# Two blocks through the first product together, with their hidden tiles kept in DRAM

## The chip, the cores and the metric

The kernel runs on one core of a Trainium2 chip. The metric is device time in microseconds (us) of one execution. The engines are named as in the profile: PE (matmuls; PEld is its weight loads), DVE (vector), ACT (scalar), POOL (GpSimd) and SP, whose queue issues nearly all DMAs.

## The reference

Linear attention, a norm over each head, and two feed-forward layers, all in float32 at the end; inputs come as 64-bit floats in DRAM.

```python
kv  = einsum('bhsd,bhse->bhde', k, v)            # 8 batches, 8 heads, 576 rows, 64 columns
out = einsum('bhsd,bhde->bhse', q, kv)
out = out / sqrt(mean(out * out, -1) + 1e-6) * g_norm
x   = out.transpose(0, 2, 1, 3).reshape(4608, 512)
h   = maximum(maximum(x @ w1, x @ w2), x @ w3)   # 512 x 768 each
x1  = h @ w_out                                  # 768 x 512
g   = s * maximum(x1 @ w_in, 0) ** 2 + b         # 512 x 2048
y   = g @ w2_out                                 # 2048 x 512
```

## The kernel before

The 4608 rows are cut into nine blocks of 512 columns (x is kept transposed): block j below 8 holds the first 512 rows of batch j, and block 8 collects the last 64 rows of all eight batches (`o_rem`). The first layer, called first and second product here, is done block by block; the second layer (lines 505 to 851) works on pairs of blocks afterwards with seven products in place of eight, and is not touched.

Every product of two float32 numbers is done as three matmuls of halves: `split` (line 91) writes a rounded high part (ACT, line 92) and the rest (line 93, on DVE or POOL), and `mm3` (line 95) issues the three matmuls (lines 96, 97, 98).

**The first product** of a block has G1 = 18 groups g: output tile m = g // 3 of h and weight matrix g % 3. `g1_part(j, g, kks)` (line 358) runs 4 x 3 = 12 matmuls of 512 columns into one of four PSUM banks of the pool `psg`; `g1_out` (line 365) copies the first of three groups to `h` (ACT) and takes the maximum with the other two (DVE, line 372); `h_split` (line 374) splits h into one of six buffers `HS` (on DVE for block 0 and for the last m, on POOL otherwise). **The second product** (`g2_mm`, line 378) has 4 groups n of 6 x 3 = 18 matmuls, in the same four banks; `g2_out` (line 385) copies them out (ACT) through the two buffers named "st" and stores them to DRAM (`x1d`).

**Weights.** The 18 tiles of w1, w2, w3 and the six of w_out are unpacked from 64-bit floats by integer and float operations: `conv_load` (line 145, DMA of 512 KB by SP), `conv_unpack` (lines 161 to 166: three operations on DVE, three on ACT), `conv_sum` (line 171, POOL), `conv_split` (lines 92 and 93, ACT and DVE). Three sets of buffers (`stages`, line 191) take turns; two of them lie in the slots that the tiles of w_out will fill later (raw tile `raw_o`). The 32 tiles of the second layer's weights pass through one stage and are stored to DRAM (`wd`, lines 496 to 501).

**Attention** of batch bb: `load_kv`, `load_rem`, `load_q`, `kv_mm` (line 243), `kv_diag`, then for each of four pairs of heads p: `q_turn` (transpose on DVE, line 278), `q_split`, `o_mm` (lines 291 to 300), `o_out` (ACT), `plan_norm` (rounding on DVE, line 318; its rest on POOL, line 319; two matmuls, lines 328 and 329; three ACT operations; three on DVE, lines 342 to 344), and `x_split` (line 348) into the block's tiles xh and xl. Batch 0 does o and the norm in full float32 without splits.

**Order.** Each step is put into `plan` with `at(pos, ...)` (line 65); `run` sorts by position and issues in that order. One unit of `pos`, called a slot here, is the time of one group of 12 matmuls; `us(t)` turns planned microseconds into slots (1 / 2.6 slot each, with t = 28 at slot 0). From slot 20 on the order on PE and SP is the planned one; below 20 only SP's, and the other engines' orders, PE's included, come from the framework's scheduling of the program. A block takes SL = 22 slots. In slots 0 to 22 block 0 runs its 18 groups, then its second product, and so on with block j from slot 22 j; batch j + 1's attention is planned beside block j. Weight tiles are planned from us(3) on, 2.6 to 3.5 planned us apart, and those of w_out 5 apart; k and v of batches 1, 2 and 3 are planned at us(19), us(34) and us(49), so ahead of slot 10.

Of the kernel before, what the change touches and what calls it, by code (L numbers as in the profile page):

```python
# [9 lines left out]
F32 = mybir.dt.float32  # L10
F32R = mybir.dt.float32r
# [9 lines left out]
P = 128  # L21
N = 512
# [7 lines left out]
def attention_max_ffn_relu2_ffn(ctx: ExitStack, tc, q, k, v, g_norm, w1, w2, w3, wo, wi, w2o, s, b, out):  # L30
# [34 lines left out]
    def at(pos, fn, *args):  # L65
        plan.append((pos, len(plan), fn, args))
# [279 lines left out]
    xs = {}  # L346

    def x_split(j, p, eng):
        if p == 0:
            xs[j] = (base.tile([P, KD, N], F32R, tag="xh", name=f"xh_{j}"),  # L350
                     base.tile([P, KD, N], F32R, tag="xl", name=f"xl_{j}"))
        split(xs[j][0][:, p], xs[j][1][:, p], st["o", j, p], eng)

# [1 line left out]

    def g1_part(j, g, kks):
        if kks[0] == 0:
            st["g1", g] = psg.tile([P, N], F32, tag="g", name=f"g1_{j}_{g}")  # L360
        xh, xl = xs[j]
        for kk in kks:
            mm3(st["g1", g], wt["w", g], slice(kk * P, (kk + 1) * P), xh[:, kk], xl[:, kk], kk == 0, kk == KD - 1)

    def g1_out(j, g):
        m, i = divmod(g, 3)
        ps = st.pop(("g1", g))
        if i == 0:
            st["h", m] = ttile(f"h_{j}_{m}")
            act(out=st["h", m], in_=ps, func=AF.Copy)  # L370
        else:
            nc.vector.tensor_tensor(out=st["h", m], in0=ps, in1=st["h", m], op=ALU.max)  # L372
# [48 lines left out]
    for p in range(NP):  # L421
# [16 lines left out]
    stages_o = [stages[0], stage(HS[M1 - 1], HS[M1 - 2], "st")]  # L438
    pos = us(3)
    for n in range(G1 + M1):  # L440
        step = 2.6 if n < 3 else 3.5 if n < 6 else 2.6 if n < 22 else 5
        plan_conv(n, pos, US)
        pos += step * US

    for j in range(NB):
        t = SL * j
        if j + 1 < B:
            bb = j + 1
            xpb = 3 if j else 2
            if bb < 4:  # L450
                kt = us(4 + 15 * bb)
                plan_kv(bb, lambda p: kt + (2 * p - 3.9) * US, lambda p: kt + 2 * p * US)
            else:
                plan_kv(bb, lambda p: t - 4 + p - 1.9, lambda p: t - 4 + p + 0.5)
            at(max(t - 10, us(20)), load_q, bb, 0, NP)
            at(t + 0.2, kv_diag, bb)
            for p in range(NP):
                a = t + 3 * p
                at(a + 0.4, q_turn, bb, p)
                if bb:  # L460
                    at(a + 1.3, q_split, bb, p)
# [3 lines left out]
                at(t + G1 + 0.2 + 0.5 * p, x_split, bb, p, nc.gpsimd if p < xpb else nc.vector)  # L465
            at(t + 13.3, o_rems, bb)
        elif j + 1 == B:
            for p in range(NP):
                a = t + 3 * p

                def sq(p=p):
                    st["o", B, p] = o_rem[:, p, :]
                    o_sq(B, p, o_rem[:, p, :])

                at(a + 0.4, sq)
                plan_norm(B, p, a + 0.5, 0.9)
                at(t + G1 + 0.2 + 0.5 * p, x_split, B, p, nc.gpsimd if p < 3 else nc.vector)
        for g in range(G1):
            if j or g >= 4:
                at(t + g, g1_part, j, g, range(KD))  # L480
            at(t + max(g, j == 0 and 3 or 0) + 1.01, g1_out, j, g)
            if g % 3 == 2:
                at(t + max(g, j == 0 and 3 or 0) + 1.25, h_split, j, g // 3)
        for n in range(KD):
            if j:
                if n < 2:
                    at(t + G1 + max(n, 0.3), g2_mm, j, n, range(M1 - 1))
                    at(t + G1 + 1.8 + 0.01 * n, g2_mm, j, n, [M1 - 1])
                else:
                    at(t + G1 + n, g2_mm, j, n, range(M1))  # L490
            at(t + G1 + max(n + 1.01, 2.01 + 0.1 * n) if j else t + G1 + 3 + 0.3 * n, g2_out, j, n)
        if not j:
            for m in range(M1):
                for n in range(KD):
                    at(t + G1 + 0.3 + m * 0.5 + 0.01 * n, g2_mm, j, n, [m])
# [383 lines left out]
```

## Time and profile before

| | |
|---|---|
| median of 3 runs | 1455.7 us (1454.43 to 1456.37) |
| profiled execution, first to last instruction (span) | 1453.9 us |
| around the span, if the profiled execution took the median's time | 1.8 us |
| PE busy (matmuls) | 1396.9 us, 96% |
| DVE busy | 951.2 us, 65% |
| ACT busy | 813.8 us, 56% |
| POOL busy | 332.7 us, 23% |
| moved by DMA | 202.63 MB, 139 GB/s in the mean |

The profiled execution's time is known by its span alone. Shares are means over the whole program; the page's second part cuts the span into 40 slices of 36 us and gives each engine's busy share in tenths (9 is 90% or more). The other views used are the stretches (busy time of each engine between two times, the granted clock of PE as a share of full speed, and the mean share of time that the DMA engines are busy, which can come out a little above 1), the timelines of single engines, and groups of instructions by line and tile. In a row of a group "x12 | 11.2, 933" means twelve instructions, 11.2 us together, 933 ns each, and behind the second bar the idle time ahead of them and what ended it.

### The profile page before, as it was taken

How to read it: one execution, taken by the hardware profiler on the slowest of the kernel's cores; microseconds unless marked ns; L12 is line 12 of the kernel's file. 1: busy time of each engine (PE TensorE's matmuls, PEld its weight loads, DVE VectorE, ACT ScalarE, POOL GpSimd, SP SyncE). 2: the span in 40 equal slices, each digit the busy share in tenths (PEclk: the TensorE clock that was granted, in tenths of full speed). 3: DMA queues.
4: the chain of work that ended last, by engine and by line, in shares of the span. 5: the costliest groups of instructions: out<-in, count | busy, mean ns of one | idle time of the engine just before them, and what ended most of it. 6: DMA issues, size and time to landing. Idle time of an engine off the chain costs nothing. (4 is left out here: it accounts for less than half of the span.)

```text
span 1453.9 us, 19580 instructions
## 1 busy us (share of the span) xinstructions
PE 1396.9 (96%) x6860; PEld 1145.0 (79%) x6860; DVE 951.2 (65%) x1439; ACT 813.8 (56%) x1454; POOL 332.7 (23%) x238
## 2 busy tenths in 40 slices
PE   4689999999999999999999999999999999999997
PEld 2467888888878788888878778988788888888887
DVE  4899473646364636446466765756877888888785
ACT  5776454445353545443365646647676666656565
POOL 1334242324232324331100000000002414141412
PEclk9789999999999999999999999999999999999999
DMA  9986244435364742213135464453676444454541
GB/s 195 198 207 106 76 65 111 111 117 102 127 91 124 113 123 58 80 29 116 65 124 202 162 230 178 142 203 127 217 265 231 132 146 174 152 175 148 176 135 40
DMA packets 229459, 202.63 MB, mean 139 GB/s; under 512 B 126320, under 2 KB 179568, under 8 KB 227184
## 3 DMA queue, kind: packets, MB, share of 16 engines
q1 hardware_dynamic: 229200, 201.11, 48.9%
q8 instruction: 54, 0.88, 0.3%
q14 instruction: 45, 0.37, 0.1%
q10 hardware_dynamic: 160, 0.26, 0.0%
HBM read 126.88 MB, written 74.45 MB: 138 GB/s over the span
## 5 line engine op out<-in xcount | busy, mean ns | idle before, releaser
L97 PE MATMUL g<-xl,w_w 128*128 128x512 f32 x648 | 255.9, 395 | 3.8 <-POOL xl L93 3.8
L96 PE MATMUL g<-xh,w_w 128*128 128x512 f32 x648 | 257.4, 400 | 0.2 <-ACT xh L92 0.2
L98 PE MATMUL g<-xh,w_w 128*128 128x512 f32 x648 | 255.6, 395 | 0.0
L92 ACT ACTIVATE zx<-z 128x512 fp32r<-128x512 f32 (+1 forms) x280 | 161.2, 586 | 123.5 <-PE zs_a L707 35.7
L629 PE MATMUL ps_a<-x_q,w_q 128*128 128x512 f32 (+1 forms) x960 | 211.1, 371 | 2.8 <-DVE cs L537 1.7
L707 PE MATMUL zs_a<-zx,w_q 128*128 128x512 f32 (+1 forms) x960 | 203.7, 369 | 0.6 <-POOL zx L93 0.3
L93 POOL TENSOR_TENSOR zx<-z,zx 128x512 fp32r<-128x512 f32 (+1 forms) x46 | 63.3, 1376 | 593.8 <-DMA gd<-cs 381.4
L629 PEld LDWEIGHTS ps_a<-x_q,w_q 128*128 128x128 f32 x960 | 167.2, 188 | 38.0 <-DVE cs L537 3.4
L93 DVE TENSOR_TENSOR zx<-z,zx 128x512 fp32r<-128x512 f32 (+1 forms) x234 | 170.6, 746 | 34.8 <-ACT zx L92 34.3
L707 PEld LDWEIGHTS zs_a<-zx,w_q 128*128 128x128 f32 x960 | 167.8, 188 | 31.9 <-POOL zx L93 0.7
L97 PEld LDWEIGHTS g<-xl,w_w 128*128 128x128 f32 x648 | 123.3, 190 | 29.7 <-POOL xl L93 4.2
L96 PEld LDWEIGHTS g<-xh,w_w 128*128 128x128 f32 x648 | 123.2, 191 | 26.8 <-issue 1.0
L98 PEld LDWEIGHTS g<-xh,w_w 128*128 128x128 f32 x648 | 123.2, 190 | 26.3
L171 POOL TENSOR_TENSOR tr_ctr<-tr_ctr,gc_cgc 128x512 int32<-128x512 int32 x42 | 56.0, 1333 | 232.4 <-DVE gc_cgc L166 169.8
L629 PE MATMUL ps_b<-x_q,w_q 128*128 128x512 f32 (+1 forms) x480 | 107.6, 372 | 1.1 <-ACT cs L640 1.0
L707 PE MATMUL zs_b<-zx,w_q 128*128 128x512 f32 (+1 forms) x480 | 103.8, 371 | 2.2 <-DVE zx L93 2.2
L372 DVE TENSOR_TENSOR h<-g,h 128x512 f32<-128x512 f32 x108 | 73.9, 684 | 42.9 <-PE g L98 42.4
L707 PEld LDWEIGHTS zs_b<-zx,w_q 128*128 128x128 f32 x480 | 83.9, 188 | 19.1 <-DVE zx L93 3.4
L629 PEld LDWEIGHTS ps_b<-x_q,w_q 128*128 128x128 f32 x480 | 83.8, 188 | 18.9 <-ACT cs L640 1.8
L96 PE MATMUL g<-h,w_o 128*128 128x512 f32 x216 | 85.7, 397 | 0.0
L162 ACT ACTIVATE tr_ctr<-raw_craw 128x512 int32<-128x512 uint32 x42 | 28.1, 669 | 102.1 <-DMA wd<-tr_ctr 86.1
L97 PE MATMUL g<-h,w_o 128*128 128x512 f32 x216 | 84.6, 392 | 0.0
(160 smaller groups left out, 2268.3 us busy)
## 6 DMA issues: line engine op xcount, KB each, us to landing
z<-gd SPq DMA_DIRECT2D x64, 512.0 KB
gd<-cs SPq DMA_DIRECT2D x96, 256.0 KB
z<-gd SPq DMA_DIRECT2D x48, 256.0 KB
x1d<-x SPq DMA_DIRECT2D x36, 256.0 KB
k<-in_k_dram SPq DMA_DIRECT2D x32, 256.0 KB
v<-in_v_dram SPq DMA_DIRECT2D x32, 256.0 KB
raw_craw<-in_moe_w_in_dram SPq DMA_DIRECT2D x16, 512.0 KB
wd<-tr_ctr SPq DMA_DIRECT2D x32, 256.0 KB
```

Of the source, the lines that this page charges most:

```text
L92: act(out=hi, in_=src, func=AF.Copy)
L93: eng.tensor_tensor(out=lo, in0=src, in1=hi.bitcast(F32), op=ALU.subtract)
L96: nc.tensor.matmul(ps, lhsT=w[:, 0, sl], rhs=xh, start=first, stop=False)
L97: nc.tensor.matmul(ps, lhsT=w[:, 0, sl], rhs=xl, start=False, stop=False)
L98: nc.tensor.matmul(ps, lhsT=w[:, 1, sl], rhs=xh, start=False, stop=last)
L162: act(out=r, in_=w32[:, :, 0], func=AF.Copy, scale=2.0 ** -29)
L171: nc.gpsimd.tensor_tensor(out=t, in0=t, in1=g.bitcast(I32), op=ALU.add)
L372: nc.vector.tensor_tensor(out=st["h", m], in0=ps, in1=st["h", m], op=ALU.max)
L629: nc.tensor.matmul(ps, lhsT=w[:, a, c], rhs=x[:, b_], start=new and k == 0 and e == 0, stop=k == HK - 1 and e == 2, skip_group_check=True)
L707: nc.tensor.matmul(ps, lhsT=w[:, a, c], rhs=x[:, b_, :n], start=new and k_ == 0 and e == 0, stop=k_ == 3 and e == 2, skip_group_check=True)
```

## The change

Blocks 0 and 1 go through the first product together. Block 0 runs groups 0 to 6 alone (`LEAD = 7`), then the groups of block 1 and of block 0 take turns (block 1's g at slot 7 + 2 g, block 0's g at 2 g - 6), until block 0 is through at slot 29; block 1's last seven groups follow to slot 36. Each finished h tile of both blocks is stored to DRAM (`h_store`, into `hd`). From slot 36 the second products of block 0 and of block 1 follow, four slots each, with m in the outer loop: their h tiles are loaded back about three slots ahead (`h_load`) and split on DVE. Block 2 begins at slot 44 as before.

With it go: block 0's x lies in four of the six `HS` buffers (block 1's in xh and xl as before), and block 1's h in the other two; the attention of batch 1 is planned at us(28) to us(46), ahead of slot 10, with its x splits on DVE, and that of batch 2 at slots 14 to 36; k and v of batches 2 and 3 are loaded beside blocks 1 and 2 in place of the head. Of the weight tiles only 0 to 3 are planned at the old pace, 4 and 5 at us(22) and us(26), tile n from 6 on four slots ahead of block 0's group n, and w_out's every two slots from slot 27. The second layer's unpacking starts at slot 44 - 2.5 in place of 28 - 2.5, spaced 4.05 in place of 4.5 slots.

```diff
+    hd = [dram.tile([P, M1, N], F32, name=f"hd{j}") for j in range(2)]
...
     def x_split(j, p, eng):
+        if not j:
+            x = pair(HS[p], f"x_{p}")
+            xs[j, p] = (x[:, 0], x[:, 1])
...
     def g1_out(j, g):
...
         if i == 0:
-            st["h", m] = ttile(f"h_{j}_{m}")
+            st["h", j, m] = ttile(f"h_{j}_{m}") if j != 1 else base.tile([P, 2, N], F32, tag=HS[M1 - 2 + m % 2],
+                                                                         name=f"h_{j}_{m}")[:, 0]
...
+    def h_store(j, m):
+        nc.sync.dma_start(out=hd[j][:, m], in_=st["h", j, m])
+
+    def h_load(j, m):
+        st["h", j, m] = (ttile if m % 2 else stile)(f"hl_{j}_{m}")
+        nc.sync.dma_start(out=st["h", j, m], in_=hd[j][:, m])
...
-        split(h[:, 0], h[:, 1], st["h", m], nc.vector if m == M1 - 1 or j == 0 else nc.gpsimd)
+        split(h[:, 0], h[:, 1], st["h", j, m], nc.vector if m == M1 - 1 or j < 2 else nc.gpsimd)
...
-        a, pr, gc = stages[n % 3] if n < G1 else stages_o[n % 2 if n < G1 + 5 else 0]
+        a, pr, gc = stages[n % 3 if n < G1 else n % 2 if n < G1 + 3 else 0]
...
+    LEAD = 7
+
+    def pos1(j, g):
+        if j:
+            return LEAD + 2 * g if g < G1 - LEAD else G1 + g
+        return g if g < LEAD else 2 * g - LEAD + 1
...
+        plan_conv(n, us((3, 5.6, 8.2, 10.8, 22, 26)[n]) if n < 6 else pos1(0, n) - 4 if n < G1 else 27 + 2 * (n - G1), US)
+
+    kt = us(19)
+    plan_kv(1, lambda p: kt + (2 * p - 3.9) * US, lambda p: kt + 2 * p * US)
+    at(us(20), load_q, 1, 0, NP)
+    at(us(28), kv_diag, 1)
+    for p in range(NP):
+        a = us(28 + 3.6 * p)
...
+        at(a + 7 * US, x_split, 1, p, nc.vector)
...
+    for j in range(2):
+        for g in range(G1):
+            t = pos1(j, g)
+            if j or g >= 4:
+                at(t, g1_part, j, g, range(KD))
+            t = max(t, 0 if j else 3)
+            at(t + 1.01, g1_out, j, g)
+            if g % 3 == 2:
+                at(t + 1.25, h_store, j, g // 3)
+        for m in range(M1):
+            t = 2 * G1 + M1 * 2 / 3 * j + 2 / 3 * m
+            at(t - 2.9, h_load, j, m)
+            at(t - 1.6, h_split, j, m)
+            for n in range(KD):
+                at(t + 0.01 * n, g2_mm, j, n, [m])
+        for n in range(KD):
+            at(2 * G1 + 4 * j + 3.8 + 0.02 * n, g2_out, j, n)
...
-        pos = SL + 6 + 4.5 * n
+        pos = 2 * SL + 4.05 * n
```

## Rows read from the trace of the kernel before

**Rows 1.** the page: its first line, and PE's busy share in 40 slices of the span

```profile
span 1453.9 us, 19580 instructions
...
PE   4689999999999999999999999999999999999997
```

**Rows 2.** busy us by stretch: PE, PEld, DVE, ACT, POOL, granted clock, DMA share, GB/s

```profile
0.00:30.00 30.00, 14.72 (x98) 8.85 (x98) 11.37 (x25) 14.24 (x28) 5.53 (x10) 1.00 0.93 188
30.00:75.00 45.00, 27.35 (x151) 18.09 (x151) 37.28 (x52) 32.30 (x56) 14.96 (x10) 0.72 1.10 208
75.00:93.00 18.00, 16.10 (x120) 12.41 (x119) 16.20 (x24) 13.70 (x26) 7.17 (x5) 0.95 0.71 163
93.00:157.00 64.00, 57.44 (x297) 45.68 (x296) 55.02 (x76) 41.09 (x73) 24.41 (x14) 0.92 0.58 126
157.00:228.00 71.00, 71.00 (x318) 58.63 (x317) 37.66 (x52) 35.58 (x61) 23.84 (x16) 1.00 0.40 86
228.00:1454.00 1226.00, 1210.32 (x5884) 1001.35 (x5882) 793.62 (x1213) 676.90 (x1213) 256.78 (x183) 1.00 0.46 139
```

**Rows 3.** timeline of PE, 100 to 230 us: start us, us, instruction, wait before it

```profile
107.80 0.69 PE L243 MATMUL kvps<-v,k 128*64 128x64 f32 x16
108.44 0.64 PE L243 MATMUL kvps<-v,k 128*64 128x64 f32 x16
...
135.92 0.79 PE L328 MATMUL ms<-sqh,ones 128*128 128x512 f32 x1 [3.39 <-DVE u L342]
...
141.63 0.40 PE L96 MATMUL g<-h,w_o 128*128 128x512 f32 x1
...
156.64 0.39 PE L96 MATMUL g<-xh,w_w 128*128 128x512 f32 x1
...
227.70 0.39 PE L96 MATMUL g<-xh,w_w 128*128 128x512 f32 x1
```

**Rows 4.** instruction groups of DVE, 0 to 153 us: x count, busy us, mean ns, idle

```profile
L166 DVE SCALAR_TENSOR_TENSOR gc_o<-raw_o,tr_o 128x512 uint32<-128x512 uint32 x12 | 11.2, 933 | 0.2
L165 DVE SCALAR_TENSOR_TENSOR tr_o<-raw_o,tr_o 128x512 int32<-128x512 uint16 x12 | 11.0, 918 | 0.8 <-ACT tr_o L162 0.8
L93 DVE TENSOR_TENSOR w_w<-tr_o,w_w 128x512 fp32r<-128x512 f32 x12 | 9.7, 804 | 2.1 <-ACT w_w L92 2.1
...
L372 DVE TENSOR_TENSOR h<-g,h 128x512 f32<-128x512 f32 x12 | 8.1, 677 | 0.0
L344 DVE SCALAR_TENSOR_TENSOR o<-o,g_sb,u 128x512 f32<-128x512 f32 x8 | 8.0, 1001 | 0.1
L278 DVE STREAM_TRANSPOSE qt<-qraw 128x576 f32<-128x576 f32 x10 | 7.5, 767 | 12.9 <-DMA qraw<-in_q_dram 12.9
L161 DVE TENSOR_SCALAR gc_o<-raw_o 128x512 uint16<-128x512 uint16 x12 | 6.7, 558 | 6.5 <-DMA raw_o<-in_moe_w_dram 6.4
L343 DVE SCALAR_TENSOR_TENSOR u<-u,y 128x512 f32<-128x512 f32 x8 | 6.5, 816 | 0.0
...
L342 DVE SCALAR_TENSOR_TENSOR u<-ms,u 128x512 f32<-128x512 f32 x8 | 5.4, 681 | 0.5 <-ACT u L336 0.5
...
L93 DVE TENSOR_TENSOR xl<-o,xh 128x512 fp32r<-128x512 f32 x4 | 4.9, 1231 | 0.1
...
L93 DVE TENSOR_TENSOR ql<-qt,qh 128x512 fp32r<-128x512 f32 x5 | 4.2, 839 | 0.0
...
L318 DVE TENSOR_SCALAR sqh<-sq 128x512 fp32r<-128x512 f32 x4 | 2.5, 618 | 0.0
```

**Rows 5.** tile raw_o, its loads on SP: ns min/median/max, first and last start us

```profile
L149 SPq DMA_DIRECT2D raw_o<-in_moe_w_dram x24: 595/608/733, 11.7 to 96.6; - x24
```

**Rows 6.** timeline of DVE around 117 us: start us, us, instruction

```profile
116.95 1.78 DVE L93 TENSOR_TENSOR w_w<-tr_o,w_w 128x512 fp32r<-128x512 f32 x1
```

**Rows 7.** timeline of POOL around 117 us: start us, us, instruction, wait before it

```profile
116.57 1.61 POOL L319 TENSOR_TENSOR sql<-sq,sqh 128x512 fp32r<-128x512 f32 x1 [0.43 <-DVE sqh L318]
```

**Rows 8.** timeline of SP around 41 us: start us, us, instruction

```profile
41.23 10.94 SPq L274 DMA_DIRECT2D qraw<-in_q_dram  x4
```

More of the change, by code (lines that the diff above doesn't have):

```diff
@@ L348, in x_split @@
     def x_split(j, p, eng):
[L349 to L352, printed above, removed]
+        if not j:
+            x = pair(HS[p], f"x_{p}")
+            xs[j, p] = (x[:, 0], x[:, 1])
+        else:
+            if p == 0:
+                xs[j] = [base.tile([P, KD, N], F32R, tag=tg, name=f"{tg}_{j}") for tg in ("xh", "xl")]
+            xs[j, p] = (xs[j][0][:, p], xs[j][1][:, p])
+        split(*xs[j, p], st["o", j, p], eng)
     hs = {}
@@ L359, in g1_part @@
         if kks[0] == 0:
-            st["g1", g] = psg.tile([P, N], F32, tag="g", name=f"g1_{j}_{g}")
-        xh, xl = xs[j]
+            st["g1", j, g] = psg.tile([P, N], F32, tag="g", name=f"g1_{j}_{g}")
         for kk in kks:
-            mm3(st["g1", g], wt["w", g], slice(kk * P, (kk + 1) * P), xh[:, kk], xl[:, kk], kk == 0, kk == KD - 1)
+            mm3(st["g1", j, g], wt["w", g], slice(kk * P, (kk + 1) * P), *xs[j, kk], kk == 0, kk == KD - 1)
     def g1_out(j, g):
         m, i = divmod(g, 3)
-        ps = st.pop(("g1", g))
+        ps = st.pop(("g1", j, g))
         if i == 0:
-            st["h", m] = ttile(f"h_{j}_{m}")
-            act(out=st["h", m], in_=ps, func=AF.Copy)
-        else:
-            nc.vector.tensor_tensor(out=st["h", m], in0=ps, in1=st["h", m], op=ALU.max)
+            st["h", j, m] = ttile(f"h_{j}_{m}") if j != 1 else base.tile([P, 2, N], F32, tag=HS[M1 - 2 + m % 2],
+                                                                         name=f"h_{j}_{m}")[:, 0]
+            act(out=st["h", j, m], in_=ps, func=AF.Copy)
+        else:
+            nc.vector.tensor_tensor(out=st["h", j, m], in0=ps, in1=st["h", j, m], op=ALU.max)
+    def h_store(j, m):
[3 more added lines that the diff above has]
+        nc.sync.dma_start(out=st["h", j, m], in_=hd[j][:, m])
     def h_split(j, m):
         h = hs[m] = pair(HS[m], f"h_{j}_{m}")
-        split(h[:, 0], h[:, 1], st["h", m], nc.vector if m == M1 - 1 or j == 0 else nc.gpsimd)
+        split(h[:, 0], h[:, 1], st["h", j, m], nc.vector if m == M1 - 1 or j < 2 else nc.gpsimd)
     def g2_mm(j, n, ms):
@@ L437, in attention_max_ffn_relu2_ffn @@
     at(us(24), o_rems, 0)
-    stages_o = [stages[0], stage(HS[M1 - 1], HS[M1 - 2], "st")]
-    pos = us(3)
     for n in range(G1 + M1):
[L441 to L446, printed above, removed]
+        plan_conv(n, us((3, 5.6, 8.2, 10.8, 22, 26)[n]) if n < 6 else pos1(0, n) - 4 if n < G1 else 27 + 2 * (n - G1), US)
+    kt = us(19)
+    plan_kv(1, lambda p: kt + (2 * p - 3.9) * US, lambda p: kt + 2 * p * US)
@@ new lines, in attention_max_ffn_relu2_ffn @@
+    at(us(20), load_q, 1, 0, NP)
+    at(us(28), kv_diag, 1)
+    for p in range(NP):
+        a = us(28 + 3.6 * p)
+        at(a, q_turn, 1, p)
+        at(a + US, q_split, 1, p)
+        at(a + 2.5 * US, o_mm, 1, p)
+        at(a + 3.2 * US, o_out, 1, p)
+        plan_norm(1, p, a + 3.5 * US, 0.45 * US)
+        at(a + 7 * US, x_split, 1, p, nc.vector)
+    at(us(44), o_rems, 1)
+    for j in range(2):
[15 more added lines that the diff above has]
+            at(2 * G1 + 4 * j + 3.8 + 0.02 * n, g2_out, j, n)
@@ L447, in attention_max_ffn_relu2_ffn @@
+    for j in range(1, NB):
+        t = SL * j if j > 1 else 14
+        d = 3 if j > 1 else 4
+        te = t + G1 if j > 1 else 2 * G1
         if j + 1 < B:
             bb = j + 1
[L449 to L455, printed above, removed]
+            plan_kv(bb, lambda p: t - 4 + p - 1.9, lambda p: t - 4 + p + 0.5)
+            at(t - (10 if j > 1 else 5), load_q, bb, 0, NP)
@@ L456, in attention_max_ffn_relu2_ffn @@
             at(t + 0.2, kv_diag, bb)
             for p in range(NP):
-                a = t + 3 * p
+                a = t + d * p
                 at(a + 0.4, q_turn, bb, p)
-                if bb:
-                    at(a + 1.3, q_split, bb, p)
+                at(a + 1.3, q_split, bb, p)
                 at(a + 3.5, o_mm, bb, p)
@@ L464, in attention_max_ffn_relu2_ffn @@
                 plan_norm(bb, p, a + 4.5, 0.9)
-                at(t + G1 + 0.2 + 0.5 * p, x_split, bb, p, nc.gpsimd if p < xpb else nc.vector)
-            at(t + 13.3, o_rems, bb)
+                at(te + 0.2 + 0.5 * p, x_split, bb, p, nc.gpsimd if p < 3 else nc.vector)
+            at(t + 4.3 + 3 * d, o_rems, bb)
         elif j + 1 == B:
@@ L477, in attention_max_ffn_relu2_ffn @@
                 at(t + G1 + 0.2 + 0.5 * p, x_split, B, p, nc.gpsimd if p < 3 else nc.vector)
+        if j < 2:
+            continue
         for g in range(G1):
-            if j or g >= 4:
-                at(t + g, g1_part, j, g, range(KD))
-            at(t + max(g, j == 0 and 3 or 0) + 1.01, g1_out, j, g)
+            at(t + g, g1_part, j, g, range(KD))
+            at(t + g + 1.01, g1_out, j, g)
             if g % 3 == 2:
-                at(t + max(g, j == 0 and 3 or 0) + 1.25, h_split, j, g // 3)
+                at(t + g + 1.25, h_split, j, g // 3)
         for n in range(KD):
[L485 to L495, printed above, removed]
+            if n < 2:
+                at(t + G1 + max(n, 0.3), g2_mm, j, n, range(M1 - 1))
+                at(t + G1 + 1.8 + 0.01 * n, g2_mm, j, n, [M1 - 1])
+            else:
+                at(t + G1 + n, g2_mm, j, n, range(M1))
+            at(t + G1 + max(n + 1.01, 2.01 + 0.1 * n), g2_out, j, n)
     for n in range(2 * M2):
-        pos = SL + 6 + 4.5 * n
+        pos = 2 * SL + 4.05 * n
         at(pos - 2.5, conv_load, ("p", n), p2_src(n), stages[0][0])
```

## The prediction, made before the changed kernel was run

> **What bounds the kernel now.** I read the page first. PE is at nine tenths or more in nearly every slice except the first three and the last [rows 1], so 1453.9 us can only shrink where PE is not yet full. The stretches show where that is [rows 2]: from 157 us to 228 us PE is busy for all of 71.00 us, and after that for 1210.32 of 1226.00 us. Before 157 us it is busy for 14.72 + 27.35 + 16.10 + 57.44 = 115.6 us, so 41 us are idle there, and some of the busy time is at the lower clock (the granted clock is 0.72 of full speed from 30 to 75 us, a mix of the levels of 1.2 and 2.4 GHz).
>
> So I follow two marks on PE's timeline [rows 3]. Block 1's first product begins at 156.64 us, block 2's at 227.70 us. The 71.06 us between them hold block 1's 288 matmuls of 512 columns (18 x 12 for the first product, 6 x 12 for the second) and 20 of block 2's attention (3 for o and 2 for the norm, four times), so one costs 71.06 / 308 = 0.231 us, its small neighbours included. Everything after block 2's start is the same work in the same order in both kernels. **The whole question is when block 2's first product begins: 227.70 us before, and then?**
>
> What holds PE back is DVE. It unpacks every weight tile (lines 161, 165, 166 and the subtraction of line 93: 0.558 + 0.918 + 0.933 + 0.804 = 3.21 us a tile [rows 4]) and does most of the attention. From 75 us on it is busy for 16.20 of 18 and 55.02 of 64 us. DMA is nearly always active too: its share is 0.93, 1.10, 0.71 in the first three stretches [rows 2], as k and v of four blocks are loaded there.
>
> **The change part by part.**
>
> *The order of the first products.* Once block 1's x is there, each weight tile feeds 24 matmuls (24 x 0.231 = 5.5 us of PE) where it fed 12 (2.8 us). DVE's share for a tile is 3.21 us of unpacking plus two thirds of a maximum for each block (line 372, 0.677 us): 4.1 us. So from that point PE, not the unpacking, sets the pace. The price is that PE has only tiles 0 to 6 of block 0 to work on until block 1's x is complete.
>
> *When is that?* DVE must do, ahead of block 1's last x, all of this by the new due times [rows 4]: nine weight tiles (0 to 8), 9 x 3.21 = 28.9 us; block 0's attention, four times line 278, 342, 343 and 344 (0.767 + 0.681 + 0.816 + 1.001 = 3.27 us, so 13.1) and two x subtractions of 1.23 on DVE, 15.5 us; block 1's attention, the same 13.1 us and four times a subtraction for q (0.839), a rounding (0.618) and an x subtraction (1.231), 23.8 us; four maxima, 2.7 us. That is 70.9 us. The first 30 us give 11.37 us of it as before, since there DVE waits for the same first loads (its idle ahead of line 278 is 12.9 us [rows 4]). 59.5 us are left. If DVE went on at its rate of 30 to 93 us, (37.28 + 16.20) / 63 = 0.85 [rows 2], they would take 70.1 us and x would be complete at 100.1 us. If it never waited: 89.5 us. I take 0.90, the rate of 75 to 93 us, as DMA is lighter then and the new order also takes k and v of blocks 2 and 3 out of this stretch: 66.1 us, so **96.1 us**.
>
> *What PE has left then:* 348 matmuls of the first products (432 less 7 x 12), 144 of the second ones, 20 of block 2's attention. Block 1's stretch of before covers 308 of these 512 with 71.06 us; the other 204 cost 47.1 us. k times v of blocks 2 and 3, which lay in the head, comes on top: two of its groups start 0.64 us apart [rows 3], eight make 5.1 us. Together 123.3 us.
>
> *The clock.* PE has little to do from about 75 to 96 us, so I expect it to start the long stretch at 1.2 GHz. A fall of this kind is in the trace: after a wait of 3.39 us PE needs 5.71 us for the 13 starts from 135.92 to 141.63 us [rows 3], where 13 x 0.231 = 3.0 would do: 2.7 us once. The Trainium skill (TensorE: Matmul & The Clock Gate, "HAM oscillation") describes a kernel that waits for its operands ahead of each piece of work and so starts each piece at the low clock. By that rule 2.7 us would be due at every such wait and not once; rows 2 agree for the head (0.72). I use it as part of a rival below.
>
> *The sum:* 96.1 + 123.3 + 2.7 = 222.1 us for block 2's start, 5.6 us before the old 227.70.
>
> *The passage of h through DRAM.* 24 transfers of 256 KB are added, 6.3 MB over some 125 us, 50 GB/s beside the 86 GB/s of 157 to 228 us; 208 were moved at the peak of the head [rows 2]. On SP each issue costs about as much as a raw load's, 0.6 us [rows 5], 15 us in all. No row shows such a passage of a hidden tile, so bounds: nothing, since h of block 0 is loaded about ten slots after its last store was due, up to 3.4 us as in the longest wait of a similar kind on PE [rows 3] where the second block's four banks are wanted 0.7 us apart while the first block's results still leave through two buffers. I take nothing, and let the 3.4 us stand in the range. SP also reads in order: see the rival.
>
> *The splits of h.* Block 1's five on POOL become DVE's. Twelve splits at 0.804 us, the last weight tile and an x subtraction are 9.6 + 3.2 + 1.2 = 14 us on DVE, while PE has 144 x 0.231 = 33.3 us of second products: hidden. If not, it would cost the 3.8 us of five splits; against that stands that POOL's work stretches a DVE subtraction to 1.78 us [rows 6, 7].
>
> *The second layer's unpacking* begins 16 slots later and is spaced 4.05 in place of 4.5 slots; its last store is due 2 slots later. DVE is busy for 793.62 of 1226.00 us there [rows 2], so this costs nothing. The loads of k, v and q for blocks 2 and 3 move likewise into a stretch with DMA share 0.40.
>
> *Running ahead.* Below slot 20 the order on PE is not written out by hand. PE may do block 0's tiles 7 and 8 while it waits for block 1's x, a gain of up to 24 x 0.231 = 5.5 us. No row decides it; I take nothing.
>
> The profiled span is 1453.9 us, 1.8 us less than the median of the runs (1455.7), which I put down to what lies around it. 1455.7 - 5.6 = 1450.1 us.
>
> **The rivals.**
>
> *DVE waits less, and the gain is larger.* With x complete at 89.5 us the sum is 215.5, 12.2 us earlier, 1443.5 us; with both tiles run ahead, 1438.0. For it: in 30 to 93 us the waits ahead of lines 161 and 278 are for loads [rows 4], and a load of q kept SP for 10.94 us [rows 8], with all of k and v behind it in the queue. Against it: the attention of one pair is a chain through PE, ACT and DVE with single buffers, whatever the load.
>
> *Nothing comes of it.* DVE keeps its 0.85: 226.1 us, 1.6 us earlier, 1454.1 us. Block 0's x is then earlier, but block 1's x takes the place of what PE waited for.
>
> *SP's order makes weight tiles late: slower.* SP now has stores of h between the loads of weights, and waits at each until PE and DVE have finished that h. Tile 12's load stands behind the stores of block 0's third h and block 1's first, tile 15's behind the next two. From there to the tile's use are six slots of 2.77 us less a maximum of 0.7 us: 15.9 us. In the trace of before the last raw load of tile 17 was issued at 96.6 us [rows 5] and its split ended at 116.95 + 1.78 us [rows 6]: 22.1 us. If that holds here, two tiles are 6.2 us late each, 12.4 us, and by the rule above each wait brings a fall of the clock, 5.4 us more: 1450.1 + 17.8 = 1467.9 us; without the clock 1462.5. It decides from about 4.3 us a tile on (8.5 us eat the gain and 0.2% besides), that is from a chain of 20 us. For it: that chain, and the load of q for block 2 in the same queue ahead. Against it: tile 17 was not urgent where it took so long, DVE did other work between.
>
> **How the numbers follow.** A measurement of this kernel can tell about 0.2%, 2.9 us, from no change. I give the larger gain 0.27, my sum 0.33 (together 0.60 faster), no change 0.15, and the late weight tiles and what is like them 0.25. The range takes in the larger gain nearly to its end, and the late tiles without most of their clock: 1437 to 1464 us.
>
> **What would show it.** In the changed kernel's timeline of PE, block 1's first matmul of the first product should start near 96 us, with PE lightly used before it; from there to block 2's first, about 126 us should pass with PE near full. DVE should be at 0.9 from 30 to 96 us. Waits of PE for weight tiles between 105 and 165 us, or raw loads whose issue on SP follows a store of h directly, would prove the slower rival; a PE timeline that shows tiles 7 and 8 of block 0 before block 1's first tile, the faster one. I am wrong in the root if block 2's start no longer sets the end, so if PE shows idle time after it that was not there before.

## The result, and the profile after

The changed kernel takes 1468.8 us (median of 4 runs, 1466.2 to 1469.6) where the kernel before takes 1455.9 on the same chip: 1.0086 of its time, 95% interval 1.0072 to 1.0100. It is slower by 0.9%; the forecast was 1450.1 us, faster.

The page of the changed kernel, its first line and PE's slices, against [rows 1]:

```profile
span 1467.8 us, 19642 instructions
...
PE   5889979999999999999999999999999999999997
```

The head is fuller than before (5, 8, 8 for 4, 6, 8), but the sixth slice, from 183 to 220 us, is now at 7 tenths. The stretches say the same, in the columns of [rows 2]; the last two lines are stretches of their own:

```profile
0.00:30.00 30.00, 15.08 (x97) 9.65 (x98) 11.37 (x25) 14.25 (x28) 5.54 (x10) 1.00 0.98 187
30.00:75.00 45.00, 36.87 (x190) 24.59 (x190) 32.98 (x51) 30.79 (x55) 12.76 (x9) 0.89 0.73 144
75.00:93.00 18.00, 15.20 (x66) 10.62 (x66) 15.78 (x25) 14.18 (x26) 6.84 (x5) 0.91 1.10 168
93.00:157.00 64.00, 58.28 (x293) 46.30 (x292) 42.30 (x62) 31.78 (x56) 13.99 (x10) 0.95 0.50 128
157.00:228.00 71.00, 59.07 (x260) 45.80 (x258) 42.88 (x60) 35.48 (x61) 16.12 (x11) 0.88 0.62 146
...
30.00:108.00 78.00, 63.44 (x352) 43.30 (x351) 58.83 (x89) 51.87 (x91) 22.65 (x15) 0.91 0.81 156
...
186.29:238.13 51.84, 42.33 (x226) 31.95 (x224) 22.84 (x32) 20.50 (x35) 8.97 (x6) 0.87 0.79 181
```

From 157 to 228 us PE was busy for all of 71.00 us before; now for 59.07, at a granted clock of 0.88. PE's timeline gives the marks, as in [rows 3]. PE takes up the last part of block 1's x at 108.03 us, the second products of blocks 0 and 1 begin at 186.29 us, block 2's first product at 238.13 us:

```profile
108.03 1.20 PE L96 MATMUL g<-xh,w_w 128*128 128x512 f32 x4 [2.26 <-ACT xh L92]
...
126.56 0.79 PE L96 MATMUL g<-x,w_w 128*128 128x512 f32 x1 [2.06 <-ACT w_w L92]
...
166.36 0.50 PE L329 MATMUL ms<-sqh,ones 128*128 128x512 f32 x1 [2.43 <-DVE u L343]
...
186.29 0.39 PE L96 MATMUL g<-h,w_o 128*128 128x512 f32 x1
...
189.10 0.50 PE L96 MATMUL g<-h,w_o 128*128 128x512 f32 x1 [1.29 <-DVE h L377]
189.44 0.39 PE L97 MATMUL g<-h,w_o 128*128 128x512 f32 x1
...
194.44 0.79 PE L96 MATMUL g<-h,w_o 128*128 128x512 f32 x1 [4.37 <-DVE h L377]
195.03 0.63 PE L97 MATMUL g<-h,w_o 128*128 128x512 f32 x1
195.46 0.63 PE L98 MATMUL g<-h,w_o 128*128 128x512 f32 x1
...
215.10 0.60 PE L96 MATMUL g<-h,w_o 128*128 128x512 f32 x1 [3.03 <-ACT x L399]
215.50 0.63 PE L97 MATMUL g<-h,w_o 128*128 128x512 f32 x1
215.93 0.63 PE L98 MATMUL g<-h,w_o 128*128 128x512 f32 x1
...
238.13 0.50 PE L96 MATMUL g<-xh,w_w 128*128 128x512 f32 x1
```

**Where the time went.** At the full clock the 144 matmuls of the second products start 0.2275 us apart, 32.8 us, and four groups of k times v add some 2.7 (an estimate; two of its groups start 0.64 us apart in [rows 3]): 35.5 us. They took 51.84, 16.3 us more. PE is busy in 42.33 of these, so 9.5 us are idle (the waits at 189.10, 194.44 and 215.10 are 8.7 of them), and 6.8 us are left. Some 5 of them are the lower clock, by a count of matmuls: 9 from 194.44 us, and 11 with one group of k times v from 215.10 us, most of them 0.43 us apart. (The granted clock of 0.87 would give 6.7 us, but from 191.45 to 194.44 us it was 0.50 while PE only waited.) The rest is small: each restart after a wait, and groups of k times v that take about 0.8 us each. Counted back by 35.5 us from 227.70, the kernel before would begin its second products at 192.2 if it did all of them last. So the changed kernel is 6 us ahead when the first products end and 10.4 us behind when block 2 starts. Another 3.5 us are lost after that (1467.8 - 238.13 = 1229.7 us to the end of the span, 1453.9 - 227.70 = 1226.2 before).

The wait of 4.37 us can be read on DVE's timeline. The maxima (line 377) free PSUM banks, and the second products, with m in the outer loop, want all four banks at once:

```profile
188.02 0.43 DVE L162 TENSOR_SCALAR gc_cgc<-raw_craw 128x512 uint16<-128x512 uint16 x1 [1.26 <-DMA raw_craw<-in_moe_w_out_dram]
188.37 0.68 DVE L377 TENSOR_TENSOR h<-g,h 128x512 f32<-128x512 f32 x1
188.97 0.68 DVE L343 SCALAR_TENSOR_TENSOR u<-ms,u 128x512 f32<-128x512 f32 x1
189.57 0.68 DVE L166 SCALAR_TENSOR_TENSOR tr_ctr<-raw_craw,tr_ctr 128x512 int32<-128x512 uint16 x1
190.16 0.68 DVE L344 SCALAR_TENSOR_TENSOR u<-u,y 128x512 f32<-128x512 f32 x1
190.77 0.68 DVE L93 TENSOR_TENSOR h<-hl,h 128x512 fp32r<-128x512 f32 x1
191.37 1.75 DVE L167 SCALAR_TENSOR_TENSOR gc_cgc<-raw_craw,tr_ctr 128x512 uint32<-128x512 uint32 x1
193.05 0.74 DVE L345 SCALAR_TENSOR_TENSOR o<-o,g_sb,u 128x512 f32<-128x512 f32 x1
193.71 0.68 DVE L377 TENSOR_TENSOR h<-g,h 128x512 f32<-128x512 f32 x1
```

DVE is not short of time there (22.84 of 51.84 us). But ahead of the maximum at 188.37 its order has an unpacking that waits 1.26 us for a raw tile of w_out, and between the last two maxima stand two more steps of unpacking, three steps of batch 2's norm and a split of h. On SP, loads stand behind other things in the same way:

```profile
100.17 14.17 SPq L380 DMA_DIRECT2D hd<-h  x2
114.43 1.28 SPq L150 DMA_DIRECT2D raw_craw<-in_moe_w_dram  x2
...
184.83 8.20 SPq L275 DMA_DIRECT2D qraw<-in_q_dram  x4
193.07 2.60 SPq L384 DMA_DIRECT2D hl<-hd  x2
```

Two stores of h hold SP for 14.17 us, and the raw weights behind them are issued at 114.43; the load of q for block 3 holds it for 8.20 us, and h of block 0 behind it comes at 193.07. The third long wait is ACT's order: the copy of x that frees PE's bank stands behind a split that waits for a reloaded h:

```profile
213.75 0.63 ACT L92 ACTIVATE h<-hl 128x512 fp32r<-128x512 f32 x1 [3.57 <-DMA hl<-hd]
214.45 0.60 ACT L399 ACTIVATE x<-g 128x512 f32<-128x512 f32 x1
```

### The profile page after: what moved, and what is told of

Read it like the earlier page. It is cut to its first block, busy times and chain, and to the rows that moved or that the text cites. A ratio compares the mean times of both kernels' runs of the same rounds, so it can differ in the third digit from the quotient of the medians.

```text
span 1467.8 us, 19642 instructions
## 1 busy us (share of the span) xinstructions
PE 1405.9 (96%) x6860; PEld 1146.4 (78%) x6860; DVE 948.3 (65%) x1446; ACT 811.6 (55%) x1454; POOL 317.8 (22%) x231
## 3 DMA queue, kind: packets, MB, share of 16 engines
q1 hardware_dynamic: 232656, 207.40, 49.2%
## 5 line engine op out<-in xcount | busy, mean ns | idle before, releaser
L96 PE MATMUL g<-xh,w_w 128*128 128x512 f32 x576 | 227.6, 397 | 2.4 <-ACT xh L92 2.3
L98 PE MATMUL g<-xh,w_w 128*128 128x512 f32 x576 | 226.6, 393 | 0.0
L97 PE MATMUL g<-xl,w_w 128*128 128x512 f32 x576 | 226.2, 393 | 0.0
L96 PEld LDWEIGHTS g<-xh,w_w 128*128 128x128 f32 x576 | 108.8, 189 | 25.8 <-ACT xh L92 3.3
L98 PEld LDWEIGHTS g<-xh,w_w 128*128 128x128 f32 x576 | 109.1, 189 | 23.3
L97 PEld LDWEIGHTS g<-xl,w_w 128*128 128x128 f32 x576 | 109.2, 190 | 22.5
L96 PE MATMUL g<-h,w_o 128*128 128x512 f32 x216 | 87.9, 407 | 9.2 <-DVE h L377 5.7
L162 DVE TENSOR_SCALAR gc_cgc<-raw_craw 128x512 uint16<-128x512 uint16 x43 | 21.0, 488 | 101.6 <-DMA raw_craw<-in_moe_w_in_dram 45.6
```

Source lines behind the costliest of these rows:

```text
L162: ts(out=c, in0=w16[:, :, 3], scalar1=0x7FFF, scalar2=None, op0=ALU.bitwise_and)
```

## The experiments

Four causes were set against each other: **SP's order** (stores of h and the load of q ahead of loads that are wanted), **DVE's order** at the hand-over to the second products, **the taking of turns** itself, and **the new place of the second layer's unpacking**. The marks of every profile stand in one table: when the first products end, how long it is from there to block 2's start (35.5 at the full clock), when block 2 starts, and the rest of the span behind it. The ratio is to runs of the kernel before on the same chip; that kernel's median beside these runs lay between 1452.4 and 1455.9 us, so small differences between two rows are read from the ratios. The marks come from one profiled execution each, and a difference of 1 or 2 us between two of them shows nothing by itself.

| run | us | ratio, 95% interval | first products end | second products | block 2 starts | rest |
|---|---|---|---|---|---|---|
| before | 1455.9 | | | | 227.7 | 1226.2 |
| changed | 1468.8 | 1.0086 (1.0072 to 1.0100) | 186.3 | 51.8 | 238.1 | 1229.7 |
| store_act | 1466.5 | 1.0078 (1.0054 to 1.0101) | 195.2 | 38.9 | 234.1 | 1231.7 |
| store_late | 1459.1 | 1.0033 (1.0024 to 1.0043) | 182.1 | 48.1 | 230.2 | 1227.3 |
| q_late | 1472.3 | 1.0120 (1.0080 to 1.0160) | 186.5 | 50.6 | 237.1 | 1230.7 |
| late2_q | 1461.0 | 1.0053 (1.0031 to 1.0074) | 184.3 | 48.3 | 232.6 | 1229.7 |
| unpack_only | 1458.1 | 1.0028 (1.0015 to 1.0042) | | | 227.0 | 1228.0 |
| wo_early | 1466.2 | 1.0087 (1.0070 to 1.0105) | 188.1 | 48.6 | 236.7 | 1228.5 |
| lead18 | 1459.0 | 1.0037 (1.0023 to 1.0050) | 182.8 | 46.8 | 229.5 | 1227.3 |
| best1 | 1461.5 | 1.0057 (1.0043 to 1.0071) | 182.9 | 46.3 | 229.1 | 1229.6 |
| handover | 1464.3 | 1.0080 (1.0064 to 1.0097) | 184.0 | 49.2 | 233.2 | 1229.3 |
| handover_lead18 | 1466.0 | 1.0084 (1.0070 to 1.0098) | 183.0 | 52.9 | 235.9 | 1228.3 |
| handover_q | 1461.6 | 1.0060 (1.0045 to 1.0075) | 185.3 | 44.9 | 230.2 | 1229.9 |
| combo | 1457.9 | 1.0022 (1.0013 to 1.0032) | 182.9 | 43.4 | 226.3 | 1229.8 |
| combo_spread | 1459.5 | 1.0033 (1.0021 to 1.0046) | 181.7 | 41.5 | 223.2 | 1233.6 |
| combo_beat | 1465.2 | 1.0081 (1.0067 to 1.0094) | 182.0 | 47.4 | 229.3 | 1231.3 |

**store_act: the stores of h leave SP's queue** and go into ACT's.

```diff
-        nc.sync.dma_start(out=hd[j][:, m], in_=st["h", j, m])
+        nc.scalar.dma_start(out=hd[j][:, m], in_=st["h", j, m])
```

> The twelve stores of h are issued from ACT's queue instead of SP's. Theory A (SP's order): in the changed kernel SP stood 60 us in front of these stores, waiting for DVE's maxima, with the loads of weights and of h behind it in the queue; of the 26 us that PE loses between block 1's last x (108 us) and block 2's start (238.1 us) at least half should go, so block 2 starts at 222 to 228 us and the time is 1452 to 1460 us. Theory B (DVE's own order and amount of work set the pace): block 2's start and the time stay within 3 us of the changed kernel's, 1466 to 1472 us.

1466.5 us: nearly nothing gained, yet everything moved. The second products run in 38.9 us with the clock at 1.00, so the passage through DRAM by itself does not make them long (columns as in [rows 2]):

```profile
195.20:234.10 38.90, 37.15 (x225) 29.04 (x224) 11.38 (x15) 12.11 (x20) 6.08 (x4) 1.00 0.41 128
```

The loss is in the first products: PE has the last of block 1's x only at 125.66 us (108.03), and SP's 60.0 us of waits for the maxima ahead of its stores have given way to other waits, 34.2 us of them for one of the raw buffers. My reading, not tried further, is that the raw weights now come earlier and DVE's order, which the framework sets, unpacks them ahead of block 1's attention.

**store_late: the stores stay on SP, but later in its order.**

```diff
-                at(t + 1.25, h_store, j, g // 3)
+                at(t + 1.25 + (2 if not j and g < 3 else 4 if g < 12 else 1), h_store, j, g // 3)
```

> The stores stay on SP but are planned later: by 2 slots for block 0's first, by 4 for most, by 1 for each block's last two, so that the weight loads planned behind them go ahead. Theory A: most of the gain of moving the stores to ACT, 1454 to 1463 us, and PE's wait for a weight tile (2.06 us at 126.6 us) gone. Theory B: 1466 to 1472 us.

1459.1 us, 9.7 less than the changed kernel (7.7 by the ratios). This and lead18, further down, are the largest effects of a single edit. PE's wait of 2.06 us for a weight tile is gone. The first products end 4.2 us sooner, the second ones take 3.7 us less, and 2.4 us less follow. So SP's order is a cause. It is not the only one: 48.1 us remain, with a wait of 4.60 us on PE at 187.53 for a copy of h.

**q_late: the load of q for block 3 six slots later.**

```diff
-            at(t - (10 if j > 1 else 5), load_q, bb, 0, NP)
+            at(t - (4 if j == 2 else 10 if j > 1 else 5), load_q, bb, 0, NP)
```

> Only the load of q for block 3 is planned 6 slots later, behind most loads of h; it kept SP for 8.2 us at 184.8 us, with seven loads of h behind it. Theory A: the second products wait less for h, block 2's start 2 to 6 us earlier, 1463 to 1467 us. Theory B: no change, 1466 to 1472 us.

1472.3 us, no gain: the wait of 4.37 us for a maximum stood ahead of it, and the q load now holds v for block 3 (a wait of 2.60 us on PE for it at 228.36). With the stores later as well (4, 2 and 0.5 slots in place of 4 and 1; **late2_q**) it is 1461.0:

> The later stores of h on SP again, but block 1's fourth by 2 slots (its buffer is wanted by the sixth h tile: ACT waited 2.66 us for that store) and the last ones by half a slot, and q of block 3 loaded 6 slots later, behind the loads of h. Theory A (whatever stands in SP's order ahead of an urgent load costs): the first two stops in the second products (4.6 and 1.2 us, with their fall of the clock) go, 3 to 7 us better than the later stores alone: 1452 to 1456 us. Theory B (DVE's order of work): the banks of the last first products are still released late, 1457 to 1461 us as with the later stores alone.

so the later q adds nothing to later stores either. Variants of this pair were of a kind: the stores on ACT's queue with the later q 1465.9 us, a lead of 10 groups 1460.3, weight tiles 1.5 slots earlier 1463.0.

**unpack_only: the kernel before, with nothing but the second layer's unpacking at its new place.**

```diff
-        pos = SL + 6 + 4.5 * n
+        pos = 2 * SL + 4.05 * n
```

> The kernel before with one part of the change alone: the second layer's unpacking starts 16 slots later and is spaced 4.05 slots. The prediction set this at nothing: within 1.5 us of the kernel before. If the 3.5 us that the changed kernel loses after block 2's start come from it, 1457 to 1459 us.

1458.1 us, 1.0028 (1.0015 to 1.0042), about 4 us of runs and 1.1 us of the profiled spans (1455.0 for 1453.9). Block 2 starts at 227.0; from there to the second layer's first matmul it takes 508.1 us (505.8 before, 509.1 in the changed kernel). This step alone, priced at nothing, costs about 4 us by the runs, 2 to 6 by the interval; its one profile shows less. Over that stretch, from block 2's start to the second layer, PE is busy for 503.71 us in the kernel before:

```profile
227.70:733.50 505.80, 503.71 (x2486) 412.35 (x2485) 263.82 (x373) 237.09 (x405) 148.76 (x105) 1.00 0.40 97
```

and in the changed one for 504.60, with 4.5 us idle in place of 2.1; most of it are waits for line 343, a step of the norm on DVE:

```profile
238.13:747.20 509.07, 504.60 (x2489) 412.14 (x2486) 271.13 (x383) 242.42 (x419) 152.61 (x108) 1.00 0.41 103
```

DVE is busy for little more than half of the stretch, and still PE waits for it: a mean share says nothing of what stands ahead of a step in DVE's order.

**wo_early: the tiles of w_out planned earlier**, so that no unpacking waits for a raw tile among the last maxima.

```diff
-... else 27 + 2 * (n - G1), US)
+... else 24.5 + 1.5 * (n - G1), US)
```

> The changed kernel with one difference: the six tiles of w_out are planned from slot 24.5 on, 1.5 slots apart (27 and 2 before). Theory A2 (the loss is in the second products, 51.8 us from 186.3 to 238.1 us where a full PE needs about 35.5: raw loads of w_out come late out of SP's order, DVE stands in its fixed order before their unpacking, and the last maxima of the first products, which free the four banks, come late behind it): second products 5 to 13 us shorter, 1456 to 1464 us. Theory B2 (the four banks and the reloading of h limit the second products whatever the weights do): second products within 3 us of 51.8, 1466 to 1471 us.

1466.2 us. The second products take 3.2 us less, but the first ones end 1.8 us later, and the interval overlaps the changed kernel's: late tiles of w_out alone are not the cause.

**lead18: no turns.** Block 0 runs all its groups, then block 1; h still goes through DRAM.

```diff
-    LEAD = 7
+    LEAD = 18
```

> The changed kernel without the interleaving: LEAD = 18 runs all of block 0's first product ahead of block 1's; the passage of h through DRAM, the earlier attention of block 1 and all else stay. If the interleaving brings what the prediction said, PE waits for weight tiles and for DVE in the first product: first products end 5 to 20 us later than 186.3 us, 1472 to 1490 us. If it is the earlier attention and the planning of weights that bring the early start of PE, and not the interleaving, the end of the first products stays within 4 us and the time within 1464 to 1473 us.

1459.0 us, 9.8 less (7.1 by the ratios). What the turns were to give is there without them: the first products end at 182.8. With the weights planned earlier (four slots ahead of block 0's groups, now one slot apart) DVE is busy for 66.21 of 78 us from 30 to 108 us, 0.85, where the changed kernel has 58.83. The places of weights and stores hang on `LEAD` too and moved with it, so this run does not part them from the turns: together, as planned here, they cost 7 to 10 us.

**best1** put together what had helped so far: later stores, a lead of 10, q at slot 41.5, w_out early, unpacking at 40 + 4.1 n.

> All repairs together: stores of h later, LEAD = 10, w_out from slot 24.5 on 1.5 apart, q of block 3 planned behind all loads of block 0's h and of k and v (slot 41.5), the second layer's unpacking from slot 40 on, 4.1 apart. Theory A2: first products end near 183 us, second products take 37 to 42 us, block 2 starts at 220 to 225 us, 2 to 7 us ahead of the kernel before, and some of the 4 us of the unpacking come back: 1448 to 1456 us. Theory B2: block 2's start stays at 229 to 231 us, 1457 to 1461 us.

1461.5 us, with block 2's start at 229.1 us as theory B2 had it, and with waits of 2.77 and 4.19 us for maxima at 187.16 and 192.32. Neither order was cleared. Ahead of the first of these maxima DVE had waited 3.44 us for a reloaded h, whose load SP issued at 181.12 us or later, behind a store of h; ahead of the second stand two splits of h and two steps of the norm.

**handover: the order at the hand-over.** The attention of batch 2 is drawn together in every engine's order, its x splits follow later, so fewer of its steps lie among the last maxima on DVE.

```diff
-        d = 3 if j > 1 else 4
+        d = 3 if j > 1 else 3.4
...
-                at(te + 0.2 + 0.5 * p, x_split, bb, p, nc.gpsimd if p < 3 else nc.vector)
+                at(te + (0.2 if j > 1 else 3) + 0.5 * p, x_split, bb, p, nc.gpsimd if p < 3 else nc.vector)
```

> The changed kernel, but in the order written for DVE the steps of the third block's attention stand closer together (3.4 slots apart, 4 before) and its x splits follow 2.8 slots later, so that fewer of them lie among the last maxima of the first two blocks' h. Theory A3: the loss at the hand-over comes from DVE's order there (the last maxima stand behind norm steps and x splits, and TensorE wants four PSUM banks at once). Then TensorE's time from the end of the first products to block 2's first product falls from 51.8 to 42 to 47 us, and the time to 1459 to 1464 us. Theory B3: the loss comes from elsewhere (the reloaded h and weight tiles, and the lower granted clock). Then that stretch stays at 50 to 53 us and the time at 1466 to 1471 us.

1464.3 us, 49.2 us for the second products: between what the two theories had, and by the ratio (1.0080 for 1.0086) no gain in time that the noise lets one see. The waits for maxima are down to 0.95 and 1.51 us, and another of the same size has come in their place on PE:

```profile
186.42 0.50 PE L96 MATMUL g<-h,w_o 128*128 128x512 f32 x1 [0.95 <-DVE h L377]
...
188.89 0.50 PE L96 MATMUL g<-h,w_o 128*128 128x512 f32 x1 [1.51 <-DVE h L377]
...
196.56 0.50 PE L96 MATMUL g<-h,w_o 128*128 128x512 f32 x1 [3.97 <-ACT h L92]
```

ACT waited 5.00 us for that h, and SP shows why: it stood behind the load of q.

```profile
182.06 7.99 SPq L275 DMA_DIRECT2D qraw<-in_q_dram  x4
190.09 2.60 SPq L384 DMA_DIRECT2D hl<-hd  x2
```

**handover_lead18** joins this to lead18 (and unpacks at 40 + 4.1 n):

> The same with no interleaving in time (the lead of the first block raised from 4 to 18 slots, so its tiles run ahead and the stores stand behind the weight loads on SP) and with the second layer's unpacking planned at 40 slots and 4.1 apart, as near to the kernel before as its place allows. Theory A3: SP's order and DVE's order at the hand-over were the two losses, and with both mended the kernel is level with the one before or ahead of it: 1450 to 1456 us. Theory B3: only SP's order was, so it stays where the lead of 18 alone put it: 1457 to 1461 us.

(`LEAD` was 7 in the changed kernel, not 4.) 1466.0 us, worse than lead18 alone, with the same wait for h (3.85 us) and 4.9 us for copies of x. Repairing the first of two causes that stand one behind the other brought nothing here.

**handover_q: handover, and q of block 3 at slot 41.5**, behind the loads of h.

> The kernel 'handover' (third block's attention steps closer together on DVE's order, its x splits later), and the load of q for block 3 planned at slot 41.5 in place of 34, so behind the loads of h on SP. In 'handover' TensorE no longer waited 4.37 us for a maximum but 3.97 us for the high part of a reloaded h, whose load stood behind the q load on SP (7.99 us). Theory A4: the loss at the hand-over is a pair of causes one behind the other (DVE's order, then SP's), and both have to go: then the second products take 42 to 45 us (51.8 in the changed kernel, 49.3 in 'handover') and the time is 1457 to 1461 us. Theory B4: a third wait of the same size stands behind these two: 47 to 50 us, 1462 to 1466 us.

Second products in 44.9 us, 6.9 less than in the changed kernel and 4.3 less than in handover; 1461.6 us, between the two forecasts of the time. The wait for the reloaded h is gone; waits of 1.10 and 2.63 us for maxima are left. So the stretch bears out the pair of causes. The later q, worth nothing in q_late, is worth 4.3 us of it once less stands among the maxima (2.7 us of the medians, where the intervals of the two ratios overlap). All repairs together with the lead of 18 (stores 1.5 and 0.5 slots later) gave 1465.5 us, none of the 1450 to 1456 hoped for: the same edits meet another order there.

**combo: handover_q with the stores of store_late.**

> Both repairs that helped, in one kernel: 'handover_q' (DVE's order at the hand-over, q of block 3 behind the loads of h) with the stores of h planned 1 to 4 slots later as in 'store_late'. Theory A5: the two losses are separate, the one in SP's order during the first products, the other at the hand-over, so the gains add: 9.7 us and 7.2 us off 1468.8 us give 1452 us, and 1450 to 1455 us is level with the kernel before. Theory B5: both gains come out of the same hand-over, where one late piece of work takes the place of another, so that little is added: 1457 to 1462 us.

1457.9 us, 1.0022 (1.0013 to 1.0032), the fastest with the change. Added in full the two gains in medians would give 1452; 10.9 of 16.9 us came. By the ratios, which take out the chip, 9.3 of 7.7 + 3.8 = 11.5 us came, and each of these is uncertain by 1 to 2 us: that anything is lost in the sum is not shown. Block 2 starts at 226.3, 1.4 us ahead of the kernel before; the 3.6 us behind it decide.

**combo_spread and combo_beat: the rest of the loss.** The unpacking at 41.5 + 4.2 n, and at 36 + 4.4 n (with w_out as in wo_early).

```diff
-        pos = 2 * SL + 4.05 * n
+        pos = 41.5 + 4.2 * n
```

> 'combo' with the second layer's unpacking begun at slot 41.5 and spaced 4.2 slots (44 and 4.05 before). In 'combo' block 2's first product begins at 226.26 us, ahead of the 227.70 of the kernel before, and the loss left lies behind it: 1229.8 us from there to the end, where the kernel before takes 1226.2. Theory A6: that loss is the density of the unpacking, whose steps stand among the norm's on DVE; a wider spacing takes back a third of it: 1228 to 1229 us behind block 2's start, 1456 to 1457.5 us in all. Theory B6: spacing matters little, what counts is which step stands by chance ahead of which: 1229 to 1231 us there, 1457 to 1459 us in all.

> 'combo' with the unpacking begun at slot 36 and spaced 4.4 slots, five of which are one block of 22 slots, so that it meets the same steps of attention in every block; the tiles of w_out are planned 2.5 slots earlier and 1.5 apart, so that the buffers are free by then. Theory A6: near the spacing of the kernel before (4.5) the loss behind block 2's start goes: 1226 to 1228 us there and 1453 to 1456 us in all, level with the kernel before. Theory B6: 1229 to 1231 us there; the earlier tiles of w_out add or take 3 us at the hand-over: 1455 to 1462 us in all.

1459.5 and 1465.2 us; neither takes the loss away. In combo_spread block 2 starts at 223.2 us, 4.5 us ahead of the kernel before, and then PE waits for the norm's steps on DVE:

```profile
270.59 0.50 PE L329 MATMUL ms<-sqh,ones 128*128 128x512 f32 x1 [2.74 <-DVE u L343]
...
283.05 0.80 PE L329 MATMUL ms<-sqh,ones 128*128 128x512 f32 x1 [3.55 <-DVE u L343]
```

Ahead of the second of these steps DVE stood 3.58 us in front of a step of the unpacking:

```profile
280.50 0.69 DVE L166 SCALAR_TENSOR_TENSOR tr_ctr<-raw_craw,tr_ctr 128x512 int32<-128x512 uint16 x1 [3.58 <-ACT tr_ctr L163]
...
282.31 0.69 DVE L343 SCALAR_TENSOR_TENSOR u<-ms,u 128x512 f32<-128x512 f32 x1
```

What is gained in front is given back behind, here where the unpacking that the change put there meets the attention. No run beat the kernel before.

## Why the prediction was wrong

**DVE's rate was too high, and the size of its work came out right by luck.** The prediction had 59.5 us of work left at 30 us ahead of block 1's x; DVE was busy for 58.83 us from 30 to 108. The rate is 58.83 / 78 = 0.75, below both 0.90 and the bound of 0.85, so PE has the last of x at 108.03 us and not at 96.1. The size agrees because two errors cancel: by 108 us DVE had unpacked twelve tiles and not nine, some 35 us in place of 28.9, and taken six maxima and not four, while most other steps were shorter than their means in [rows 4]. Part of the delay is thus work that the sum had later. I took DVE to wait less because DMA would be lighter. The DMA share was lower, 0.81 from 30 to 108 us for 0.98 before, but DVE's waits in this stretch say otherwise:

```profile
DVE gc_o L162 <- DMA raw_o<-in_moe_w_dram: 6.5, 6, 2.2
DVE gc_cgc L162 <- DMA raw_craw<-in_moe_w_dram: 4.5, 3, 2.6
DVE u L343 <- ACT u L337: 4.3, 2, 2.1
```

(us in total, times, longest): 11.0 us for raw weights, which are planned later here, and 4.3 us in the chain of the norm.

**Running ahead was real and larger.** I took it as nothing, 5.5 us at most. By 108.03 us PE had done 156 matmuls of the first products, not 84: ten groups of block 0, and 36 matmuls of block 1 with the parts of x that were there. That is read from the groups of PE from 30 to 108 us (lines 96 and 98 have as many as line 97; x is block 0's, xl block 1's):

```profile
L97 PE MATMUL g<-x,w_w 128*128 128x512 f32 x40 | 17.7, 443 | 0.0
...
L97 PE MATMUL g<-xl,w_w 128*128 128x512 f32 x12 | 4.8, 402 | 0.0
```

The 72 more are 72 x 0.231 = 16.6 us. PE was not lightly used before block 1's x either: 15.20 of 18 us from 75 to 93.

**The late x and the running ahead cancel.** The forecast of 222.1 us for block 2, less 35.5 us, means an end of the first products at 186.6 us; it was 186.29. In the account: 12 us late, 16.6 us ahead, 4.5 us of waits at 126.56 and 166.36. The gain that I forecast was there at this mark, but by luck, since the size of neither error was foreseen.

**The step that failed is the passage of h through DRAM** ("I take nothing", at most 3.4 us), with the splits of h called hidden under 33.3 us of second products. The stretch took 16.3 us too long, nearly five times the bound. The bound itself was misread: the 3.39 us of [rows 3] are a wait of the norm's matmul for DVE, not for a bank or a hidden tile, and by the plan block 0's last h is stored at slot 29.25 and loaded at 36.4, seven slots later and not ten. I looked for a late reload, and for each engine's share. What happens is that last maxima, reloaded h, w_out, batch 2's norm and q meet within 30 us, and that each queue works in its order: DVE, SP and ACT each in turn hold PE. store_act (38.9 us) and combo_spread (41.5 us, with a DMA share of 0.76 as against 0.79) show that the transfers as such take little; handover and handover_q show the order.

**The clock falls more than once.** I had 2.7 us once. In the first products it fell behind the waits of 2.26, 2.06 and 2.43 us that ended at 108.03, 126.56 and 166.36. In the second, after the wait of 4.37 us the matmuls start 0.43 us apart, 1.2 GHz, until 198.02 us, and again after the 3.03 us at 215.10; after the 1.29 us at 189.10 they go on at 0.23 us, 2.4 GHz. Together some 5 us in this stretch. The Trainium skill (TensorE: Matmul & The Clock Gate, "HAM oscillation") tells of a kernel in which every piece of work behind a long wait for its operands starts at the low clock; the trace agrees for the waits of 4.37 and 3.03 us, and the short one of 1.29 us brought no fall.

**"So this costs nothing" was wrong for the unpacking**: 3.5 us behind block 2's start in the profiles, and about 4 us (2 to 6) for the unpacking alone in the runs of unpack_only. I said that I should be wrong in the root if PE were idle there where it wasn't before; it is, by 2.4 us.

**The slower rival had the time and half of the mechanism.** It gave 1467.9 us (1468.8 measured), by SP's order, and store_late confirms that order: 9.7 us, 7.7 by the ratios. But its place was wrong. Two weight tiles were to be 6.2 us late each between 105 and 165 us; PE waits 2.06 us for one. The nearness of its number is partly chance: the sum that came true is 1450.1 - 0.3 + 16.3 + 3.5 = 1469.6 us, most of it at a hand-over that no case of mine had.

**What stays open:** whether the gains of store_late and handover_q add in full, what the turns cost apart from the places of weights and stores, and how much of the 3.5 us behind block 2's start is the unpacking and how much the phase in which it meets the attention. With three other starts and spacings the rest of the span was between 1228.3 and 1233.6 us, with the changed kernel's own it was between 1227.3 and 1231.7, and each of these runs had a block 2 that began at another time.

## What to carry to other kernels

Where a change makes several streams meet at one place (here the end of one product, the start of the next, and a reload), write down for each in-order queue what stands ahead of the step that PE wants, and price that; shares of busy time and counts of bytes show none of it. When one wait is taken away, look at once for the one of the same size behind it, and test the repairs in pairs: the later load of q showed nothing alone and 4 us of its stretch after another repair. A step moved "into a stretch with room" is priced by who waits for the steps that it lands among.

## What the runs showed of the hardware that was not expected

How long PE stays at the lower clock after a wait differs. In the changed kernel it was back at 198.02 us, 3.6 us after the wait of 4.37 us had ended. In store_late, whose timeline of PE this is, it took some 10 us, with one more wait of 1.24 us in between:

```profile
187.53 0.65 PE L96 MATMUL g<-h,w_o 128*128 128x512 f32 x1 [4.60 <-ACT h L375]
187.97 0.63 PE L97 MATMUL g<-h,w_o 128*128 128x512 f32 x1
...
191.92 0.79 PE L96 MATMUL g<-h,w_o 128*128 128x512 f32 x1 [1.24 <-DVE h L377]
...
197.63 0.56 PE L97 MATMUL g<-h,w_o 128*128 128x512 f32 x1
198.02 0.40 PE L98 MATMUL g<-h,w_o 128*128 128x512 f32 x1
```

The starts are 0.43 us apart up to 197.63 us and 0.23 us behind. At 0.2 us a matmul the fall cost under 2 us in the one place (8 starts) and some 4 us in the other (20 starts). Nor does the fall stand at the wait's end each time: in the changed kernel, after the 2.43 us that ended at 166.36, the next matmuls start 0.23 us apart until 167.39, and the starts 0.43 us apart run from 168.53 to 170.66.
